# Attention in steps of two key tiles, q and k transposed on the host, and each engine's order written out

## The chip, the core and the metric

The kernel runs on one NeuronCore of a Trainium2 chip. Its time is the device time of one execution in microseconds, the median of the runs; lower is better. The engines are PE (TensorE), DVE (VectorE), ACT (ScalarE), POOL (GpSimd) and SP (SyncE, which here only issues DMAs); PEld in a profile is PE's loading of weights.

## The reference

Attention with a block mask over 4 batches of 8 heads, 768 positions and 64 columns a head, then a feed-forward network (FFN) over all 3072 tokens:

```python
def _attn_ref(q, k, v, sampled_blocks):
    B, H, S, D = q.shape
    scores = (1.0 / np.sqrt(D)) * np.matmul(q, k.transpose(0, 1, 3, 2))
    ...
    mask = np.abs(blk_i - blk_j) <= 1
    mask = mask | (blk_i == 0) | (blk_j == 0) | (blk_i == n_blocks - 1) | (blk_j == n_blocks - 1)
    ...
    scores = np.where(mask, scores, -1000000000.0)
    scores = scores - np.max(scores, axis=-1, keepdims=True)
    attn = np.exp(scores)
    attn = attn / (np.sum(attn, axis=-1, keepdims=True) + 1e-09)
    return np.matmul(attn, v)

def _moe_ref(x, w_in, w_out):
    h = x @ w_in
    g = h - np.tanh(h)
    return g @ w_out
```

Blocks are of 32 positions; where lines are left out, the block numbers are worked out and three sampled key blocks are allowed for each query block. The two weight matrices are 512 × 2048 and 2048 × 512.

## The kernel before

**Attention.** Two heads make a pair; there are 16. The scores are computed transposed, keys on partitions: for a key tile of 128 rows, PE multiplies it with all 768 queries (`qk_exp`, L270). Products keep fp32 accuracy by splitting each operand into a high part (rounded by ACT) and a low part (the rest), and the mask and the row maximum enter the product as 25 more rows. Four operand areas per pair (`sA` to `sD`, in one of three `slots`) hold these rows; the maxima for a query tile come from a product of its own (`smax`, L252), are reduced by DVE (L253), turned by PE (L258), negated (L260) and sent by DMA into a row of `sB` (L261), which the scores then need (L277).

For one key tile: PE writes the scores to PSUM (L276, L277), ACT takes the exponential to SBUF, `pe` (L279), ACT or DVE rounds it to fp16, `ph` (L289, L287), POOL or DVE subtracts it, `pl` (L291), and PE accumulates both with v (L306, L312, L313, eighteen multiplications). Of twelve key tiles of a pair, DVE takes two `ph` and one `pl`. After six key tiles DVE normalizes the head (`norm`, L321 to L325) and a finished pair is written to DRAM (`spill`).

q and k come untransposed. For each pair PE turns them with twelve transposes into PSUM (L192), ACT takes the high parts (L194), DVE the low parts (L195), and twelve DMAs of 192 KB (`dist`, L207) spread them over the operand areas. v is scaled by a power of two and split by ACT (L237) and DVE (L238).

**PSUM.** Of the eight banks, six form three buffers of 1024 columns (`big`: turned q and k, maxima, scores), and two are single banks (`one`: accumulators, small turns, the first FFN products).

**The FFN.** 96 units, each a tile of 512 tokens with 128 hidden columns: 12 multiplications into a PSUM bank (L527), tanh and a polynomial on ACT and DVE (L534 to L549), the low part on POOL (L550), 12 multiplications out (L559 to L561). Weights come as 64-bit words, converted by three DVE operations (L426, L429, L432) and split in two parts. The weights of the first three hidden tiles are converted during the attention; two more loads (L414, L418) are issued at the very start. Two units (`ffn.step`) are written inside the attention stage, on `one`.

**Order.** Every piece of work is put in a list with a time (`at`, L340), and the list is sorted; a scheduler then orders each engine's instructions by its own simulation, within the dependencies, so that the order on an engine isn't the order of the list.

## Time and profile before

| | |
|---|---|
| runs | 995.37, 996.8, 991.48 us; median 995.37 |
| the profiled execution | 990.7 us span |
| PE, DVE, ACT, POOL busy | 930.6, 742.5, 627.5, 458.4 us |
| DMA | 99.78 MB, 101 GB/s over the span |

The span reaches from the first to the last instruction of the profiled execution. The attention lasts to about 436 us, the FFN from there to the end. Shares of the whole span are means over both: what bounds the attention is to be read from its own stretches of time. The page's slices:

```profile
PE   5888998999899999878999999999999999999997
DVE  5699787888788888868999876766676666666664
ACT  1566787888688888745666665564565555555553
POOL 1566677777677777853454522222222222222221
PEclk9999999999999999998999999999999999999999
DMA  9988677677667777214451220210020000001001
```

Each digit is one of 40 slices of 24.8 us, in tenths. PE is the busiest in both stages; POOL's work is nearly all in the first 18 slices, where the attention is.

### The profile page before, as it was taken

The page shows a single profiled execution, that of the slowest core. Times are in us where ns is not written, and L with a number is a line of the kernel's source. Part 1 is how long each engine was busy: PE and PEld are TensorE (multiplying, and loading weights), DVE is VectorE, ACT ScalarE, POOL GpSimd, SP SyncE. Part 2 cuts the span into 40 slices and gives each one's busy share as a digit, 9 for nine tenths or more (in the row PEclk, how much of TensorE's full clock was granted, in tenths as well). Part 3 has the DMA queues.
Part 4 walks back from the last instruction along what each step waited for, and adds up shares of the span by engine and source line. Part 5 has one row for each costly group of instructions (what it writes and reads, how often), then busy time and mean ns, then how long its engine had stood idle before and what let it go on. Part 6 is the DMA issues. An engine that isn't in the chain of part 4 may idle for free.

```text
span 990.7 us, 18571 instructions
## 1 busy us (share of the span) xinstructions
PE 930.6 (94%) x7264; PEld 776.5 (78%) x7264; DVE 742.5 (75%) x1120; ACT 627.5 (63%) x943; POOL 458.4 (46%) x308
## 2 busy tenths in 40 slices
PE   5888998999899999878999999999999999999997
PEld 4666887888788888766878878888888888888885
DVE  5699787888788888868999876766676666666664
ACT  1566787888688888745666665564565555555553
POOL 1566677777677777853454522222222222222221
PEclk9999999999999999998999999999999999999999
DMA  9988677677667777214451220210020000001001
GB/s 234 253 228 200 158 165 161 153 167 172 137 160 168 175 165 182 85 32 154 128 187 50 79 75 11 94 35 12 1 75 1 1 22 22 1 1 43 1 1 42
DMA packets 74695, 99.78 MB, mean 101 GB/s; under 512 B 6008, under 2 KB 63544, under 8 KB 74608
## 3 DMA queue, kind: packets, MB, share of 16 engines
q1 hardware_dynamic: 74608, 98.60, 39.2%
q8 instruction: 57, 0.93, 0.4%
q14 instruction: 30, 0.25, 0.1%
HBM read 44.64 MB, written 15.20 MB: 60 GB/s over the span
## 4 chain that ended last, share of the span: by engine, by line
PE 70%; DMA 12%; DVE 9%; ACT 3%; issue 3%; SPq 1%; POOL 1%; ACTq 0%; DVEq 0%; POOLq 0%
PE pf L527 25%; PE pf L559 8%; PE pf L560 8%; PE pf L561 8%; DMA slot<-nm 7%; PE st L276 4%; PE st L277 4%; PE sm L252 3%; DVE mc L253 2%; PE av L313 2%; PE av L312 1%; DMA slot<-hiq 1%; PE av L306 1%; DMA slot<-hik 1%; DVE ph L287 1%
## 5 line engine op out<-in xcount | busy, mean ns | idle before, releaser
L291 POOL TENSOR_TENSOR pl<-pe,ph 128x768 f16<-128x768 f32 x173 | 290.6, 1693 | 132.1 <-ACT ph L289 80.9
L550 POOL TENSOR_TENSOR gl<-t,gh 128x512 fp32r<-128x512 f32 x96 | 124.1, 1293 | 362.9 <-ACT gh L549 304.9
L253 DVE TENSOR_REDUCE mc<-sm 128x1 f32<-128x768 f32 x192 | 181.2, 952 | 64.0 <-PE sm L252 62.6
L279 ACT ACTIVATE pe<-st 128x768 f32<-128x768 f32 x192 | 154.5, 807 | 86.6 <-PE st L277 77.7
L542 DVE TENSOR_TENSOR t<-t,pf 128x512 f32<-128x512 f32 x94 | 64.6, 687 | 123.8 <-ACT t L536 123.7
L276 PE MATMUL st<-slot 128*128 128x512 f32 (+1 forms) x384 | 144.6, 377 | 6.2 <-DVE mc L253 5.4
L277 PE MATMUL st<-slot 89*128 89x512 f32 (+1 forms) x384 | 127.9, 353 | 10.8 <-DMA slot<-nm 10.8
L549 ACT ACTIVATE gh<-t 128x512 fp32r<-128x512 f32 x96 | 60.6, 631 | 120.7 <-DVE t L546 120.7
L289 ACT ACTIVATE ph<-pe 128x768 f16<-128x768 f32 x154 | 129.6, 843 | 3.7
L313 PE MATMUL av<-vhl,pl 128*128 128x65 f16 x1152 | 129.3, 194 | 2.0 <-POOL pl L291 1.7
L312 PE MATMUL av<-vhl,ph 128*128 128x64 f16 x1152 | 129.0, 195 | 0.0
L306 PE MATMUL av<-vhl,ph 128*128 128x65 f16 x1152 | 128.5, 195 | 0.0
L252 PE MATMUL sm<-slot 88*128 88x512 f32 (+1 forms) x384 | 113.3, 381 | 13.5 <-DMA slot<-hiq 7.3
L313 PEld LDWEIGHTS <-pl 128*128 128x128 f16 x1152 | 107.0, 99 | 14.8 <-issue 8.2
L306 PEld LDWEIGHTS <-ph 128*128 128x128 f16 x1152 | 107.6, 97 | 4.4 <-issue 1.3
L312 PEld LDWEIGHTS <-ph 128*128 128x128 f16 x1152 | 108.3, 98 | 1.5 <-issue 0.8
L534 ACT ACTIVATE u<-pf 128x512 f32<-128x512 f32 x94 | 56.2, 598 | 82.0 <-PE pf L527 81.6
L276 PEld LDWEIGHTS st<-slot 128*128 128x128 f32 x384 | 75.4, 196 | 25.8 <-DVE mc L253 7.2
L277 PEld LDWEIGHTS st<-slot 89*128 89x128 f32 x384 | 76.1, 198 | 24.0 <-DMA slot<-nm 14.8
L252 PEld LDWEIGHTS sm<-slot 88*128 88x128 f32 x384 | 63.1, 204 | 17.8 <-issue 5.7
L546 DVE COPY_PREDICATED t<-mk,pf 128x512 f32<-128x512 int32 x94 | 69.8, 743 | 6.9 <-DVE pf L545 0.5
L559 PE MATMUL pf<-wx,gh 128*128 128x512 f32 x192 | 74.7, 389 | 0.0
(123 smaller groups left out, 1981.4 us busy)
## 6 DMA issues: line engine op xcount, KB each, us to landing
slot<-hik SPq DMA_DIRECT2D x64, 192.0 KB
slot<-hiq SPq DMA_DIRECT2D x64, 192.0 KB
stage<-w_in SPq DMA_DIRECT2D x13, 512.0 KB
stage<-w_out SPq DMA_DIRECT2D x13, 512.0 KB
rawk<-k SPq DMA_DIRECT2D x16, 384.0 KB
...
```

The source lines that it names most:

```text
L252: nc.tensor.matmul(pm[:, c], lhsT=sB[s][0:88, j, t * P : (t + 1) * P], rhs=sA[s][0:88, j, c], start=True, stop=True)
L253: maxed.append(nc.vector.tensor_reduce(out=mcs[h][:, t : t + 1], in_=pm[:, 0:S], op=ALU.max, axis=AX.X))
L276: nc.tensor.matmul(st[:, c], lhsT=sC[s][:, j, kc], rhs=sD[s][:, j, c], start=True, stop=False)
L277: nc.tensor.matmul(st[:, c], lhsT=sA[s][0:89, j, kc], rhs=sB[s][0:89, j, c], start=False, stop=True)
L279: nc.scalar.activation(out=pe, in_=st[:, 0:S], func=AF.Exp, scale=0.125)
L289: nc.scalar.activation(out=ph, in_=pe, func=AF.Copy)
L291: d = eng.tensor_tensor(out=pl, in0=pe, in1=ph, op=ALU.subtract)
L306: m = nc.tensor.matmul(o[:, to, :], lhsT=ph[:, c], rhs=vv[:, 0:65], start=(kt == 0 and t == 0), stop=False, skip_group_check=True)
L312: nc.tensor.matmul(o[:, to, 0:64], lhsT=ph[:, c], rhs=vv[:, 65:129], start=False, stop=False, skip_group_check=True)
L313: nc.tensor.matmul(o[:, to, :], lhsT=pl[:, c], rhs=vv[:, 0:65], start=False, stop=last, skip_group_check=True)
L527: nc.tensor.matmul(h, lhsT=w[:, cc], rhs=x[:, c, :], start=(k == 0), stop=(k == 3 * NCT - 1))
L559: nc.tensor.matmul(o, lhsT=gh[:, c], rhs=wo[0][ft], start=(ft == f0), stop=False)
```

## The change

The host hands over q and k already transposed, as one array of [pair, 128, 2, 768], and v in tile order. PE's transposes of q and k and their PSUM buffers go; ACT takes the high part of both from SBUF in one operation (L133), and POOL the low part, where DVE took it from PSUM (L141).

A step now takes two key tiles. Scores go to one fixed area of three banks (`pst`), maxima to another (`psm`), accumulators to one bank, small turns to one; each is a single buffer. The exponential (L256), the rounding (L260), the subtraction (L266) and the reduction of the maxima (L226) have 1536 columns; all rounding is on ACT and all subtraction on POOL. `pe` has two buffers, `ph` and `pl` four. Multiplications are as many as before, but for the columns at which they are cut. The accumulation of a step stands after the scores and the maxima of the step two later.

At the end of the stage, `in_order` chains every engine's instructions, SP's DMAs included, in the order of the list, so that the scheduler has no choice there. The conversion of the first weights is cut into its three operations, one a pair; `split_w` runs on DVE alone; the two loads of L414 and L418 move from the start to step 91; the first two FFN units use banks of `psm`. The output rows of a tile are adjacent. The first pair has paths of its own.

```diff
+def in_order(tc, start):
+
+    last = {}
+    for i in tc.nc.cur_bb.bb.instructions[start:]:
+        if i.engine in last:
+            tc.add_manual_dep(
+                i,
+                last[i.engine].name,
+                mybir.DependencyInfo(mybir.DependencyClass.NoSync, mybir.DependencyReason.DATA),
+                reason="order",
+            )
+        last[i.engine] = i
+
...
-        big = actx.enter_context(tc.tile_pool(name="ps_big", bufs=3, space=PSUM))
-        one = actx.enter_context(tc.tile_pool(name="ps_one", bufs=2, space=PSUM))
...
-        )
-        ffn.big, ffn.one = ps
...
+    ps = ctx.enter_context(tc.tile_pool(name="ps", bufs=1, space=PSUM))
+    pst = ps.tile([P, W2], F32, name="pst")
+    psm = ps.tile([P, W2], F32, name="psm")
+    pav = ps.tile([P, 512], F32, name="pav")
+    pmisc = ps.tile([P, 512], F32, name="pmisc")
...
+    def high(pr, x=None):
+        if pr == 1:
+            hms[pr] = [p2.tile([P, 1024], F32R, tag="wraw", name=f"hm1{x}")[:, 0:S] for x in range(2)]
+        elif pr not in hms:
+            t = p2.tile([P, 2, S], F32R, tag="hm", name=f"hm{pr}", bufs=1)
+            hms[pr] = [t[:, 0], t[:, 1], t.bitcast(F32)]
+        if pr > 1:
+            nc.scalar.activation(out=t, in_=raws[pr], func=AF.Copy)
+        else:
+            for x in range(2):
+                nc.scalar.activation(out=hms[pr][x], in_=raws[pr][:, x], func=AF.Copy)
+
+    def low(pr):
+        los[pr] = p2.tile([P, 2, S], F32R, tag="lo", name=f"lo{pr}", bufs=1)
+        if pr > 1:
+            nc.gpsimd.tensor_tensor(out=los[pr], in0=raws[pr], in1=hms[pr][2], op=ALU.subtract)
...
+    def direct(dst, x):
+        nc.vector.tensor_copy(out=dst[0][0:64, 0], in_=hms[0][x].bitcast(F32)[0:64])
+
+    def dist(pr, dst, r0, src, x, j):
+        nc.sync.dma_start(
+            out=dst[pr % NSLOT].bitcast(F32)[r0 : r0 + 64, j], in_=(src[pr][x] if src is hms else src[pr][:, x]).bitcast(F32)[64 * j : 64 * j + 64]
+        )
...
-    def prep_qk(pr, nm):
-        raw = loads[pr][0 if nm == "k" else 1]
-        hi = p2.tile([P, 2, HS], F32R, tag="hi" + nm, name=f"hi{nm}{pr}", bufs=1)
-        lo = p2.tile([P, 2 * HS], F32R, tag="lo" + nm, name=f"lo{nm}{pr}", bufs=1).rearrange("p (j c) -> p j c", j=2)
-        pt = big(f"pt{nm}{pr}")
-        for j in range(2):
-            for u in range(3):
-                c = (3 * j + u) * P
-                nc.tensor.transpose(pt[:, c : c + P], raw[:, j, 2 * u : 2 * u + 2, :].rearrange("p r d -> p (r d)"), ident)
-        ptv = pt[:, 0:S].rearrange("p (j c) -> p j c", j=2)
-        nc.scalar.activation(out=hi, in_=ptv, func=AF.Copy)
-        nc.vector.tensor_tensor(out=lo, in0=ptv, in1=hi.bitcast(F32), op=ALU.subtract)
-        hl[pr, nm] = hi, lo
...
-        pm = big(f"sm{h}_{t}")
-        for c in (slice(0, 512), slice(512, S)):
-            nc.tensor.matmul(pm[:, c], lhsT=sB[s][0:88, j, t * P : (t + 1) * P], rhs=sA[s][0:88, j, c], start=True, stop=True)
-        maxed.append(nc.vector.tensor_reduce(out=mcs[h][:, t : t + 1], in_=pm[:, 0:S], op=ALU.max, axis=AX.X))
...
+        for x in range(2):
+            t = 2 * i + x
+            for c in ((0, 512), (512, 768)) if x == 0 else ((0, 256), (256, 768)):
...
+    def maxima(h, i, ps=psm):
+        nc.vector.tensor_reduce(
+            out=mcs[h][:, 2 * i : 2 * i + 2], in_=ps.rearrange("p (x s) -> p x s", x=2), op=ALU.max, axis=AX.X
+        )
...
-        st = big(f"st{h}_{kt}")
-        kc = slice(kt * P, (kt + 1) * P)
-        for c in (slice(0, 512), slice(512, S)):
-            nc.tensor.matmul(st[:, c], lhsT=sC[s][:, j, kc], rhs=sD[s][:, j, c], start=True, stop=False)
-            nc.tensor.matmul(st[:, c], lhsT=sA[s][0:89, j, kc], rhs=sB[s][0:89, j, c], start=False, stop=True)
-        pe = p2.tile([P, S], F32, tag="pe", name=f"pe{h}_{kt}", bufs=4)
-        nc.scalar.activation(out=pe, in_=st[:, 0:S], func=AF.Exp, scale=0.125)
-        pes[h, kt] = pe
-
-    def split(h, kt):
-        pe = pes.pop((h, kt))
-        ph = p2.tile([P, S], F16, tag="ph", name=f"ph{h}_{kt}", bufs=PB)
-        pl = p2.tile([P, S], F16, tag="pl", name=f"pl{h}_{kt}", bufs=PB)
-        if (h * T + kt) % 12 in (PH_DVE if h < HPH else PH_DVE_END):
-            nc.vector.tensor_copy(out=ph, in_=pe)
-        else:
-            nc.scalar.activation(out=ph, in_=pe, func=AF.Copy)
-        eng = nc.vector if (h * T + kt) % 12 in (PL_DVE if h < HPL else PL_DVE_END) else nc.gpsimd
-        d = eng.tensor_tensor(out=pl, in0=pe, in1=ph, op=ALU.subtract)
-        plin[h, kt] = d
...
+        for x in range(2):
+            kc = slice((2 * i + x) * P, (2 * i + x + 1) * P)
+            for c in ((0, 512), (512, 768)) if x == 0 else ((0, 256), (256, 768)):
+                o = pst[:, x * S + c[0] : x * S + c[1]]
+                q = slice(*c)
+                nc.tensor.matmul(o, lhsT=sC[s][:, j, kc], rhs=sD[s][:, j, q], start=True, stop=False)
+                nc.tensor.matmul(o, lhsT=sA[s][0:89, j, kc], rhs=sB[s][0:89, j, q], start=False, stop=True)
+
+    def expo(s_):
+        pes[s_] = p2.tile([P, W2], F32, tag="pe", name=f"pe{s_}", bufs=2)
+        nc.scalar.activation(out=pes[s_], in_=pst, func=AF.Exp, scale=0.125)
+
+    def p_high(s_):
+        ph = p2.tile([P, W2], F16, tag="ph", name=f"ph{s_}", bufs=4)
+        nc.scalar.activation(out=ph, in_=pes[s_], func=AF.Copy)
+        phs[s_] = ph
+
+    def p_low(s_):
+        ph = phs[s_]
+        pl = p2.tile([P, W2], F16, tag="pl", name=f"pl{s_}", bufs=4)
+        nc.gpsimd.tensor_tensor(out=pl, in0=pes.pop(s_), in1=ph, op=ALU.subtract)
+        phs[s_] = ph, pl
...
+    def accum(s_):
...
+        ph, pl = phs.pop(s_)
+        for x in range(2):
+            kt = 2 * i + x
...
+                nc.tensor.matmul(oav[:, t, :], lhsT=ph[:, c], rhs=vv[:, 0:65], start=(kt == 0 and t == 0), stop=False, skip_group_check=True)
...
+    k = -76
+    for c, j in ((CD[:2], 0), (AB, 1), (CD[2:], 0)):
+        for d in c:
+            at(k, dist, 0, *d, j)
...
+    for s in range(NSTEP):
+        at(s, scores, s)
+        at(s + 0.02, expo, s)
+        at(s + 0.12, p_high, s)
+        at(s + 0.2, p_low, s)
+        at(s + 2.5, accum, s)
+    for h in range(NHEAD):
+        if h >= 2:
+            for i in range(3):
+                at(3 * h - 6 + i + 0.1, smax, h, i)
+                at(3 * h - 6 + i + 0.11, maxima, h, i)
+            at(3 * h - 3 + 0.05, turn_max, h)
+            at(3 * h - 3 + 0.07, neg_max, h)
+        at(3 * h + 5.03, norm, h)
...
+        load_w(nc, wraw[m, ft], w_in, w_out, m, ft)
...
+    for x in range(6 * NPRE):
+        m, ft, n = "io"[x // 3 % 2], x // 6, x % 3
+        s = 6 * x + 10 if x < 13 else 77 + x
+        if n == 0:
+            at(s - 4.5 if x < 15 else 87, load_pre, m, ft)
+        at(s + 0.04, convert_pre, m, ft, n)
...
+    ffn.one = one
     for j in range(CT):
-        at(X0 + DX * j, x_first, j)
+        at(84.3 + 0.4 * j, x_load, j)
+        at(90.06 + j, x_turn, j)
...
-        at(F0 + DF * i + 2, ffn.split_w, i)
+        at(90.2 + 0.4 * i if i < 2 else 94.3, ffn.fetch_w, i)
+        at(92.04 + i if i < 2 else 96.3, ffn.split_w, i)
...
+        at(91.5 + 0.3 * i, ffn.stage_w, i)
...
+        at(95.6 + i, ffn.step)
     ev.sort(key=lambda e: e[:2])
     for _, _, f, args in ev:
         f(*args)
+    in_order(tc, start)
...
-            self.parts(lo.bitcast(F32), hi, lo, self.nc.vector if ft < 2 and x else self.nc.gpsimd)
+            self.parts(lo.bitcast(F32), hi, lo, self.nc.vector)
...
-                nc.sync.dma_start(out=self.out[b * S : (b + 1) * S, :].rearrange("(p t) d -> t p d", t=T)[t], in_=ob)
+                nc.sync.dma_start(out=self.out[b * S + t * P : b * S + (t + 1) * P, :], in_=ob)
...
-    block = (col % P * T + np.array(TORD)[col // P]) // BLK
+    block = col // BLK
...
+    kq = np.stack([inputs["k"], inputs["q"]]).reshape(2, NPAIR, 2, S, D).transpose(1, 2, 4, 0, 3).reshape(NPAIR, P, 2, S)
+    vt = inputs["v"].reshape(NPAIR, 2, T, P, D).transpose(0, 3, 1, 2, 4).reshape(NPAIR, P, 2 * T * D)
```

PE in the middle of the attention. Before, around the scores of a key tile (`st`), with head and tile in the names (`ptk11` is pair 11's turned k, `pmt20` head 20's turned maxima, `av18` an accumulator):

```order
L312 MATMUL av18_4616<-vhl0_103,ph18_5_4702 128x64
L313 LDWEIGHTS pl18_5_4703
L313 MATMUL av18_4616<-vhl0_103,pl18_5_4703 128x65
L306 LDWEIGHTS ph18_5_4702
L306 MATMUL av18_4616<-vhl0_103,ph18_5_4702 128x65
L192 MATMUL ptk11_4764<-ident_64,rawk11_4187 128x128
L258 MATMUL pmt20_4690<-ident_64,mc20_4514 6x128
L192 MATMUL ptk11_4764<-ident_64,rawk11_4187 128x128 x5
L312 LDWEIGHTS ph18_5_4702
L312 MATMUL av18_4616<-vhl0_103,ph18_5_4702 128x64
```

The transposes stand between multiplications of one accumulation. After, the end of an accumulation (of step 1), and the scores and maxima that follow it:

```order
L283 MATMUL pav_102<-vhl0_104,pl1_268 128x65
L251 MATMUL pst_100<-slot0_73 128x512
L252 MATMUL pst_100<-slot0_73 128x512
L251 MATMUL pst_100<-slot0_73 128x256
L252 MATMUL pst_100<-slot0_73 128x256
L251 MATMUL pst_100<-slot0_73 128x256
L252 MATMUL pst_100<-slot0_73 128x256
L251 MATMUL pst_100<-slot0_73 128x512
L252 MATMUL pst_100<-slot0_73 128x512
L216 MATMUL psm_101<-slot1_74 128x512
L216 MATMUL psm_101<-slot1_74 128x256 x2
L216 MATMUL psm_101<-slot1_74 128x512
```

The transposes are gone, and scores and maxima of two tiles stand in one run, then the next accumulation.

POOL in the first pairs. Before, it does nothing in the attention but subtractions (head and key tile in the names):

```order
L291 TENSOR_TENSOR pl8_2_2234<-pe8_2_2160,ph8_2_2233 128x768
L291 TENSOR_TENSOR pl8_3_2249<-pe8_3_2175,ph8_3_2248 128x768
L291 TENSOR_TENSOR pl8_4_2307<-pe8_4_2231,ph8_4_2306 128x768
L291 TENSOR_TENSOR pl8_5_2337<-pe8_5_2246,ph8_5_2336 128x768
L291 TENSOR_TENSOR pl9_0_2389<-pe9_0_2304,ph9_0_2388 128x768
```

After, with the low part of a pair's q and k among them (steps in the names of `pl`, pairs in those of `lo`):

```order
L141 TENSOR_TENSOR lo4_883<-raw4_690,hm4_814 128x1536
L266 TENSOR_TENSOR pl12_944<-pe12_929,ph12_941 128x1536
L266 TENSOR_TENSOR pl13_1003<-pe13_993,ph13_1001 128x1536
L266 TENSOR_TENSOR pl14_1069<-pe14_1054,ph14_1067 128x1536
L266 TENSOR_TENSOR pl15_1134<-pe15_1120,ph15_1132 128x1536
L266 TENSOR_TENSOR pl16_1197<-pe16_1182,ph16_1192 128x1536
L266 TENSOR_TENSOR pl17_1261<-pe17_1243,ph17_1259 128x1536
L141 TENSOR_TENSOR lo5_1263<-raw5_1071,hm5_1194 128x1536
L266 TENSOR_TENSOR pl18_1324<-pe18_1309,ph18_1321 128x1536
```

Once in six steps the low part stands between two subtractions. ACT some pairs later, after:

```order
L260 ACTIVATE ph22_1573<-pe22_1562 128x1536
L133 ACTIVATE hm6_1575<-raw6_1451 128x1536
L256 ACTIVATE pe23_1624<-pst_100 128x1536
L260 ACTIVATE ph23_1640<-pe23_1624 128x1536
L256 ACTIVATE pe24_1692<-pst_100 128x1536
L260 ACTIVATE ph24_1704<-pe24_1692 128x1536
L197 ACTIVATE vhl2_106<-rawv5_1423,sb5_1631 128x12x64
L256 ACTIVATE pe25_1756<-pst_100 128x1536
L260 ACTIVATE ph25_1764<-pe25_1756 128x1536
L256 ACTIVATE pe26_1817<-pst_100 128x1536
```

The high part of the next q and k stands between a rounding and the next exponential, and so does, two steps later, the scaled v.

The end of the attention on PE. Before, around the first FFN products (`h0_0`, `h0_1`) and the first turn of the FFN (`pf6`):

```order
L312 MATMUL av31_7628<-vhl0_103,ph31_3_7624 128x64
L527 MATMUL h0_0_7665<-slot1_74,slot2_75 128x512 x12
L313 LDWEIGHTS pl31_3_7625
...
L313 MATMUL av31_7628<-vhl0_103,pl31_5_7700 128x65
L527 MATMUL h0_1_7739<-slot1_74,slot2_75 128x512 x12
L441 MATMUL pf6_7859<-ident_64,slot1_74 128x128 x4
L527 MATMUL pf4_7857<-slot1_74,slot2_75 128x512 x12
```

After, with the step's number in `pl`:

```order
L283 MATMUL pav_102<-vhl0_104,pl93_6066 128x65
L583 MATMUL psm_101<-slot1_74,slot2_75 128x512 x12
L281 LDWEIGHTS ph94_6116
...
L283 MATMUL pav_102<-vhl0_104,pl94_6118 128x65
L583 MATMUL psm_101<-slot1_74,slot2_75 128x512 x12
L281 LDWEIGHTS ph95_6173
...
L283 MATMUL pav_102<-vhl0_104,pl95_6175 128x65
L497 MATMUL pf6_6400<-ident_64,slot1_74 128x128 x4
L583 MATMUL pf4_6398<-slot1_74,slot2_75 128x512 x12
```

Both units stand ahead of the last accumulation, where the second stood behind it.

SP's queue at the start, after; the load of the pair 2's q and k (`raw2`) is its row 21:

```order
L150 DMA slot1_74<-hm10_147 64x768
L150 DMA slot1_74<-hm11_148 64x768
L150 DMA slot0_73<-hm0_132 64x768 x2
L150 DMA slot0_73<-lo0_138 64x768 x2
L150 DMA slot1_74<-hm10_147 64x768
L150 DMA slot1_74<-hm11_148 64x768
L175 DMA slot2_75<-st_sb_111 24x2x768
L175 DMA slot2_75<-mk_112 24x2x768
L120 DMA raw2_199<-qk 128x1536
L150 DMA slot1_74<-hm10_147 64x768
L150 DMA slot1_74<-hm11_148 64x768
L150 DMA slot1_74<-lo1_185 64x768 x2
```

Loads, fills and distributions of the pairs 0 and 1 stand ahead of it.

More of the change, by code (lines that the diff above doesn't have):

```diff
@@ L44 @@
 NPRE = 3
[L45 removed]
 NV = 3
[L47 to L63 removed]
+XF = 8
+NH0 = 2
+HIMASK = -4096
 THR2 = 0.16
@@ L130, in load @@
-    def load(pr, which="kqv", first=None):
-        b, hp = divmod(pr, H // 2)
-        r = loads.setdefault(pr, [])
-        for nm, src in ((n, x) for n, x in (("k", k), ("q", q), ("v", v)) if n in which):
-            t = p2.tile([P, 2, T, D], F32, tag="raw" + nm, name=f"raw{nm}{pr}", bufs=2)
-            d = nc.sync.dma_start(out=t, in_=src[b, 2 * hp : 2 * hp + 2].rearrange("h (p t) d -> p h t d", t=T))
-            r.append(t)
-            if pr <= 3 and first is not None:
-                after(first, d)
```

375 lines of the change are left out of this document (186 added, 189 removed).

## The prediction, made before the changed kernel ran

> **What bounds the kernel now.** I read the busy shares and the chain first, to see which engine and which of its waits set the end; then windows of one steady pair, to get the pace; then single rows.
>
> ```profile
> span 990.7 us, 18571 instructions
> PE 70%; DMA 12%; DVE 9%; ACT 3%; issue 3%; SPq 1%; POOL 1%; ACTq 0%; DVEq 0%; POOLq 0%
> 0.00:60.00 60.00, 42.58 (x342) 33.89 (x343) 40.17 (x63) 26.27 (x33) 22.80 (x20) 1.00 0.91 232
> 60.00:120.00 60.00, 51.83 (x603) 42.53 (x604) 52.44 (x78) 40.19 (x51) 39.46 (x22) 0.94 0.78 197
> ...
> 285.00:309.00 24.00, 22.74 (x305) 19.63 (x304) 19.64 (x29) 19.50 (x26) 18.08 (x11) 1.00 0.71 167
> 285.00:309.00 24.00, 9.68 (x12) 1.00 0.71 167
> ```
>
> A window row gives the stretch, its length, the busy time of PE, PEld, DVE, ACT and POOL, then the granted PE clock, the DMA share and GB/s; the last row is the same stretch counting only the exponentials (L279). Twelve exponentials are one pair of heads, so a pair takes 24.0 us in the middle of the attention, PE is busy for 22.7 of them, and POOL only for 18.1. In the first 60 us DMA is the limit (0.91 of its engines, 232 GB/s); the row of 60 to 120 still shows it at 0.78.
>
> ```profile
> L291 POOL TENSOR_TENSOR pl<-pe,ph 128x768 f16<-128x768 f32 x173 | 290.6, 1693 | 132.1 <-ACT ph L289 80.9
> L550 POOL TENSOR_TENSOR gl<-t,gh 128x512 fp32r<-128x512 f32 x96 | 124.1, 1293 | 362.9 <-ACT gh L549 304.9
> L253 DVE TENSOR_REDUCE mc<-sm 128x1 f32<-128x768 f32 x192 | 181.2, 952 | 64.0 <-PE sm L252 62.6
> L279 ACT ACTIVATE pe<-st 128x768 f32<-128x768 f32 x192 | 154.5, 807 | 86.6 <-PE st L277 77.7
> L289 ACT ACTIVATE ph<-pe 128x768 f16<-128x768 f32 x154 | 129.6, 843 | 3.7
> L534 ACT ACTIVATE u<-pf 128x512 f32<-128x512 f32 x94 | 56.2, 598 | 82.0 <-PE pf L527 81.6
> ```
>
> These are groups: line, operation and shape, then total busy us and mean ns of one, then the idle time before them and who ended it. ACT and DVE wait for PE; POOL waits for ACT. So PE sets the pace of the steady attention, with 1.3 us of gaps per pair.
>
> **PE's part.** The timeline of PE, start and length:
>
> ```profile
> 257.47 0.48 PE L276 MATMUL st<-slot 128*128 128x512 f32 x1
> ...
> 258.26 0.51 PE L252 MATMUL sm<-slot 88*128 88x512 f32 x2
> 258.61 0.21 PE L313 MATMUL av<-vhl,pl 128*128 128x65 f16 x1
> ...
> 259.30 0.71 PE L192 MATMUL ptk<-ident,rawk 128*128 128x128 f32 x5
> 259.84 0.19 PE L312 MATMUL av<-vhl,ph 128*128 128x64 f16 x1
> ...
> 431.55 0.20 PE L313 MATMUL av<-vhl,pl 128*128 128x65 f16 x1
> ...
> 432.05 0.19 PE L306 MATMUL av<-vhl,ph 128*128 128x65 f16 x1
> 432.08 0.19 PE L312 MATMUL av<-vhl,ph 128*128 128x64 f16 x1
> ```
>
> Recorded lengths overlap, so I take start to start. Scores of one key tile take 258.26 − 257.47 = 0.79 us, maxima 0.35, and the eighteen accumulating matmuls from 431.55 to 432.08 take 18/17 of 0.53, or 0.56. A step of two tiles is therefore 2 × (0.79 + 0.35 + 0.56) = 3.40 us, and a pair of six steps 20.4. The change issues exactly these multiplications again, with other column cuts. Five transposes last 0.54 us (259.30 to 259.84), so the twelve that go take 1.3 us per pair. If PE still set the pace, a pair would fall from 24.0 to about 20.4 + 0.3 for the two small turns + the gaps of today, 1.3: 22.0. That would be 2 us × about 14.5 steady pairs = 29 us.
>
> **What else can set the pace.** Two rows of single lines, with minimum, median and maximum ns and the first and last start:
>
> ```profile
> L279 ACT ACTIVATE pe<-st x192: 784/811/815, 31.6 to 431.6; 128x768 f32<-128x768 f32 x192
> L237 ACT ACTIVATE vhl<-rawv,sb x16: 933/936/947, 34.9 to 403.9; 128x768 f16<-128x768 f32 x16
> ```
>
> ACT: the slope of one element is (807 − 598)/256 = 0.82 ns, so a 1536-column exponential is 807 + 768 × 0.82 = 1.43 us and its rounded copy 0.843 + 0.63 = 1.47. Six steps are 17.4, the one high part of q and k adds 1.47, the scaled v 0.94: 19.8 of ACT, below PE. DVE: six reductions at 2 × 0.95 less one start, about 1.8 each, 10.8 instead of today's 11.4, and it loses its rounded copies, its low parts of q, k and one subtraction; DVE is no bound. Moving those copies to ACT is hidden under the waits of 86.6 us that ACT has before L279.
>
> POOL is the resource that changes most. It took eleven of twelve 768-column subtractions; now it takes every one, as six of 1536 columns, and the low part of q and k besides. The before trace has no 1536-column POOL operation. From below, its slope is that between its two shapes, (1693 − 1293)/256 = 1.56 ns, so 1.69 + 768 × 1.56 = 2.89; the undisturbed minimum of 1.635 (its row is below) against the same 1.293 makes 1.34 ns and 2.66. From above it is twice the undisturbed median, 3.30. I take 3.1, nearer to the upper end, because two operations of its own line are the nearest row, less one start. The low part has the types of L550: from below 1.293 + 1024 × 1.34 = 2.66, from above 3 × 1.293 = 3.88; I take 3.4 by the same reasoning. POOL per pair: 6 × 3.1 + 3.4 = 22.0, bounds 18.6 to 23.7. POOL thus becomes as long as PE's 22.0, and comes ahead of it with any loss.
>
> The Trainium skill, "GPSIMD Engine Reference", section "3.1 Elementwise — side-by-side cycle accounting", gives 4497 ns for a two-input fp32 operation of 2048 columns, which scaled to 1536 is an estimate of 3.37 us; by that the sum would be 6 × 3.37 + 3.4 = 23.6 per pair, and no run here has that shape.
>
> **Two losses on POOL.** First, the buffers. There are two `pe` tiles, so exponential s+2 waits for subtraction s, and then 1.43 + 1.47 must pass on ACT before subtraction s+2 can start, while POOL has only subtraction s+1, 3.1, to do: even, with 0.2 to spare. The 1.47 of the q and k copy and the 0.94 of v, once a pair each, stand on ACT between a rounded copy and the next exponential, and in this kernel nothing may overtake them. Up to 2.4 us per pair would show as a hole on POOL; its 3.4 us low part, which needs no exponential, fills part. From 0 to 2.4, I take 1.2.
>
> Second, a lock between DVE and POOL:
>
> ```profile
> L291 POOL TENSOR_TENSOR pl<-pe,ph x173: 1635/1650/2622, 33.4 to 433.6; 128x768 f16<-128x768 f32 x173
> L238 DVE SCALAR_TENSOR_TENSOR vhl<-rawv,sb,vhl x16: 1019/1020/2397, 37.8 to 405.5; 128x768 f16<-128x768 f32 x16
> 60.78 2.62 POOL L291 TENSOR_TENSOR pl<-pe,ph 128x768 f16<-128x768 f32 x1 [5.15 <-ACT ph L289]
> 61.22 0.68 DVE L432 SCALAR_TENSOR_TENSOR cvto<-rawo,cvto 128x512 int32<-128x512 int32 x1
> 61.83 2.40 DVE L238 SCALAR_TENSOR_TENSOR vhl<-rawv,sb,vhl 128x768 f16<-128x768 f32 x1
> ```
>
> A subtraction that starts at 60.78 while DVE is at operations with two SBUF inputs lasts 2.62 instead of 1.65: it ends 1.5 after DVE's at 61.90. DVE's v low part, 1.02 alone, then lasts 2.40, to 64.23: 0.83 after POOL is done at 63.40. They take turns. In the changed kernel DVE keeps one such v low part per pair and one part of a weight conversion (0.68), so up to 1.02 + 0.68 = 1.7 us of POOL per pair goes to them; where they fall into POOL's holes it is nothing. I take half, 0.8. DVE's wait, up to 3 us behind a 1536-column operation, holds the reduction queued behind it, and so PE's next maxima; DVE, busy for 19.6 of 24 us now and for less then, has room to catch up.
>
> The Trainium skill, "SBUF — State Buffer", section "🔬 SBUF: two separate sides", says that GpSimd and such a DVE operation hold a shared port pair exclusively for the whole instruction, whichever starts first. This trace agrees (2.62 against 1.65); by the rule the whole 1.7 would be lost in every pair, 0.9 × 14.5 = 13 us more than I take, and without it nothing.
>
> Sum per pair: 22.0 + 1.2 + 0.8 = 24.0, against 24.0 now. So the 29 us of PE are, by my reading, eaten by POOL: the steady stretch comes out even.
>
> **Front.** Pair 0 needs fewer steps before its first exponential: no transposes, no 1 MB of weights at the head of the queue (at 232 GB/s that is 4.5 us), so I expect it at 24 to 27 instead of 31.6. But the second exponential stands behind the high part of pair 2 on ACT, whose load is row 21 of the queue. Up to it stand three loads of q and k (0.79 MB each by their shapes), fourteen distributed pieces (0.197), six fills (0.147), v (0.39) and the tables (0.08): 6.5 MB, 28 us at 232 GB/s, so the second exponential comes at about 33 to 36. Distribution traffic per pair is the same, twelve pieces of 192 KB. I take 0, from −6 to +6.
>
> **Tail.**
>
> ```profile
> 431.58 0.81 ACT L279 ACTIVATE pe<-st 128x768 f32<-128x768 f32 x1 [1.25 <-DVE rs L321]
> 434.25 4.57 PE L527 MATMUL h<-slot,slot 128*128 128x512 f32 x12 [1.97 <-DVE xq L325]
> 443.18 0.73 DVE L546 COPY_PREDICATED t<-mk,h 128x512 f32<-128x512 int32 x1
> 447.60 0.60 ACT L534 ACTIVATE u<-h 128x512 f32<-128x512 f32 x1 [3.02 <-PE h L527]
> 452.47 1.09 PE L441 MATMUL pf<-ident,slot 128*128 128x128 f32 x4 [4.91 <-issue]
> 452.48 0.69 DVE L426 TENSOR_SCALAR pf<-stage 128x512 int32<-128x512 int32 x1
> 434.00:439.00 5.00, 4.75 (x23) 3.68 (x24) 2.01 (x2) 0.14 (x1) 1.20 (x1) 0.66 0.00 0
> ```
>
> Today unit 0 of the FFN waits for the last but one normalization (1.97 us), runs at a clock of 0.66 and takes 4.57; unit 1 must wait for head 31's normalization and ends at 447.6, and the first transposes and the first conversion come at 452.5, 20.9 us after the last exponential. After the change both units stand between the last accumulations and use the bank of the maxima, free by then. Last exponential + 1.43 + 1.47 + 3.1 is +6.0; two port waits behind DVE's weight splits, about +2; accumulation +1.1: +9.1. Then either the turn follows at once (11.8 us saved), or, if both units' element work on DVE (twice five operations of 0.7 as L546's) comes first, 7 us later, and 4.8 are saved. I take 9, nearer to the first, since unit 0's element work can run beside the accumulations. From there the FFN is untouched, and its pace passes the shift on.
>
> Sum: 0 + 0 − 9 against the span of 990.7 gives 981.7. The median of the runs, 995.37, lies 4.7 above that span, outside it or by run; I add this: 986.4.
>
> **Rivals.**
> (A) The forecast, POOL about level with today's pace: 986.
> (B) POOL's long operation is cheap (2.66 for both shapes, 18.6 per pair) or the port turns fall into holes. Then PE bounds at 22.0: −29 − 9 plus 4 for losses at the front, 961. For it: POOL's 1.3 ns slope from its own rows. Against it: rows of two dtypes can't give a clean slope.
> (C) Slower: POOL at its upper price, 6 × 3.2 + 3.6 = 22.8, plus 1.6 of holes and 1.2 of turns, 25.6 per pair. That is +1.6 × 14.5 = 23, − 9: 1009. It decides where POOL's total with losses passes 24.6 per pair, for there the tail's 9 us are spent. For it: 2.62 and 2.40 above. Against it: POOL sat idle 132.1 us before L291, some of which was slack that can be used. PE's gaps, 24.0 − 20.7, cost nothing as long as its clock stays above 0.86; the row of 434 to 439 shows 0.66 after a wait of 2 us, and if that happened after each hole, C would come sooner.
> (D) The pace is even and the tail's gain does not arrive, because the conversions and not the units set the FFN's start: 995.
>
> **How the numbers follow.** A 0.42, B 0.24, C 0.24, D 0.10. The predicted time is A's 986.4. B reaches below 961 only if the holes vanish as well, C above 1013 only at both upper prices, so 958 to 1013 holds eight in ten. A's own range, from half the tail gain lost (+4.5) to a POOL 0.4 us per pair cheaper (−5.8), is 981 to 991. 0.5%, or 5 us, is about what a measurement can tell from no change: below 990.4 lie B and most of A, 0.54; above 1000.4 C and a little of D, 0.26; the rest is 0.20.
>
> **What would show it.** Right: POOL busy above 21 of each 24 us, its 1536-column mean between 2.9 and 3.3, ACT's exponentials waiting for POOL's subtraction instead of PE, and the transposes ahead of unit 2 some 12 us after the last exponential, not 20.9. Wrong: PE at over 95% in steady windows (B), a pair over 25 us or stretched v low parts of 3 us and more in every pair (C), a first exponential before 25 followed by a hole beyond 12 us (front mis-sized), or a first conversion still 20 us behind the last exponential (D).

## The result and the profile after

The change makes the kernel slower: 1032.76 us (1023.37 to 1044.67, 4 runs) against 993.42, ratio 1.0315, interval 1.0266 to 1.0364. Two of its four runs, 1039.29 and 1044.67, fell in a slower state of the chip at a lower clock; the ratio and its interval leave them out. The profiled execution has a span of 1021.6 us, 30.9 more than before. Starts of exponentials and of the first conversion of the FFN, from the two timelines, divide that:

| stretch | before | after | difference |
|---|---|---|---|
| start to exponential of tile 24, step 12 | 90.1 | 95.7 | +5.6 |
| from there to tile 168, step 84 (twelve pairs) | 297.1 | 321.1 | +24.0 |
| to the last exponential | 44.4 | 44.2 | −0.1 |
| to the first conversion | 20.9 | 19.6 | −1.2 |
| to the end | 538.2 | 540.9 | +2.6 |

Tiles and steps are counted from 0. So nearly four fifths of the loss lie in the steady attention: 26.8 us per pair against 24.8 (the 24.0 of the prediction was one of the quicker pairs). One window of 240 us, before and then after, with the columns of the prediction's windows:

```profile
120.00:360.00 240.00, 226.51 (x2982) 196.37 (x2979) 192.83 (x295) 193.78 (x246) 177.43 (x108) 0.99 0.72 160
```

```profile
120.00:360.00 240.00, 209.36 (x2618) 178.02 (x2618) 179.00 (x175) 172.23 (x124) 201.18 (x63) 0.90 0.62 159
```

PE's share fell from 94% to 87%, POOL's rose from 74% to 84%, and no engine is full. PE's granted clock fell from 0.99 to 0.90, so part of PE's 87% is slower work. The costs, in the views by group and by single line:

```profile
L266 POOL TENSOR_TENSOR pl<-pe,ph 128x1536 f16<-128x1536 f32 x96 | 308.9, 3226 | 72.5 <-ACT ph L260 52.4
...
L266 POOL TENSOR_TENSOR pl<-pe,ph x96: 3095/3122/3847, 32.6 to 464.2; 128x1536 f16<-128x1536 f32 x96
L141 POOL TENSOR_TENSOR lo<-raw,hm x14: 3472/3488/3507, 47.7 to 394.2; 128x1536 fp32r<-128x1536 f32 x14
L473 DVE TENSOR_SCALAR cvti<-rawi x3: 3211/3220/3226, 85.5 to 408.1; 128x512 int32<-128x512 int32 x3
L477 DVE SCALAR_TENSOR_TENSOR cvto<-rawo,cvto x3: 2992/3322/3481, 199.4 to 452.8; 128x512 int32<-128x512 int32 x3
L473 DVE TENSOR_SCALAR pf<-stage x26: 680/689/706, 480.7 to 592.6; 128x512 int32<-128x512 int32 x26
L201 DVE SCALAR_TENSOR_TENSOR vhl<-rawv,sb,vhl x16: 1010/2818/3926, 30.7 to 420.7; 128x768 f16<-128x768 f32 x16
```

POOL's prices are what was forecast (3.12 and 3.49). New are DVE's lengths: a conversion operation, 0.69 in the FFN, takes 3.2 to 3.5 us in the attention in the median, v's low part 2.8, where it took 1.02 before. What one such wait does, in the timelines of POOL, DVE, PE and ACT (start, length, idle time before and its releaser):

```profile
157.08 9.96 POOL L266 TENSOR_TENSOR pl<-pe,ph 128x1536 f16<-128x1536 f32 x3
...
157.38 3.63 DVE L201 SCALAR_TENSOR_TENSOR vhl<-rawv,sb,vhl 128x768 f16<-128x768 f32 x1 [1.33 <-ACT vhl L197]
160.94 1.74 DVE L225 TENSOR_REDUCE mc<-psm 128x2 f32<-128x1536 f32 x1
...
162.74 1.01 PE L216 MATMUL psm<-slot 88*128 88x512 f32 x4 [2.32 <-DVE mc L225]
...
167.95 1.45 ACT L256 ACTIVATE pe<-pst 128x1536 f32<-128x1536 f32 x1 [4.48 <-PE pst L252]
...
171.05 3.12 POOL L266 TENSOR_TENSOR pl<-pe,ph 128x1536 f16<-128x1536 f32 x1 [4.01 <-ACT ph L260]
```

DVE's v low part starts just after a subtraction and gets on only when that is over; the reduction behind it starts 3.6 us late; PE's next maxima wait for the single buffer that this reduction reads, and behind them, in the fixed order, the accumulation and the next scores; ACT waits 4.48, and in the end POOL itself 4.01. After its wait PE is also slower for a while. The window rows before and behind the wait:

```profile
155.00:160.40 5.40, 5.39 (x69) 4.36 (x65) 4.07 (x2) 5.14 (x4) 5.27 (x3) 1.00 0.84 199
163.00:168.00 5.00, 5.00 (x50) 4.40 (x50) 2.32 (x2) 0.52 (x2) 4.04 (x2) 0.66 0.66 150
```

The granted clock is 0.66 there instead of 1.00, and from the first multiplication of an accumulation to the last one of the scores behind it PE takes 3.8 us instead of 2.6.

### The profile page after: what moved, and what is told of

Read it like the earlier page. It is cut to its first block, busy times and chain, and to the rows that moved or that the text cites. A ratio compares the mean times of both kernels' runs of the same rounds, so it can differ in the third digit from the quotient of the medians.

```text
span 1021.6 us, 17486 instructions
## 1 busy us (share of the span) xinstructions
PE 923.3 (90%) x7072; PEld 768.4 (75%) x7072; DVE 721.3 (71%) x939; ACT 630.7 (62%) x775; POOL 527.2 (52%) x245
## 4 chain that ended last, share of the span: by engine, by line
PE 61%; DVE 19%; ACT 6%; issue 4%; POOL 1%; DMA 1%; SPq 0%; DVEq 0%; ACTq 0%; POOLq 0%
PE pf L583 23%; PE pf L615 8%; PE pf L616 8%; PE pf L617 8%; DVE mc L225 6%; PE psm L216 3%; ACT pe L256 3%; PE pst L251 3%; DVE vhl L201 3%; PE pst L252 3%; PE pav L281 2%; PE pav L283 1%; POOL pl L266 1%; PE pav L282 1%; DVE am L179 1%
## 5 line engine op out<-in xcount | busy, mean ns | idle before, releaser
L266 POOL TENSOR_TENSOR pl<-pe,ph 128x1536 f16<-128x1536 f32 x96 | 308.9, 3226 | 72.5 <-ACT ph L260 52.4
L256 ACT ACTIVATE pe<-pst 128x1536 f32<-128x1536 f32 x96 | 138.7, 1445 | 119.3 <-PE pst L252 96.1
L225 DVE TENSOR_REDUCE mc<-psm 128x2 f32<-128x1536 f32 x94 | 164.7, 1753 | 39.2 <-PE psm L216 39.0
L251 PE MATMUL pst<-slot 128*128 128x512 f32 (+1 forms) x384 | 143.6, 392 | 14.5 <-ACT pe L256 13.6
L216 PE MATMUL psm<-slot 88*128 88x512 f32 (+1 forms) x376 | 96.1, 382 | 55.2 <-DVE mc L225 44.5
L260 ACT ACTIVATE ph<-pe 128x1536 f16<-128x1536 f32 x96 | 142.6, 1485 | 2.9
L283 PE MATMUL pav<-vhl,pl 128*128 128x65 f16 x1152 | 130.3, 201 | 5.0 <-POOL pl L266 4.8
L252 PE MATMUL pst<-slot 89*128 89x512 f32 (+1 forms) x384 | 132.9, 364 | 0.0
L281 PE MATMUL pav<-vhl,ph 128*128 128x65 f16 x1152 | 131.7, 203 | 0.5 <-DVE xq L294 0.5
L282 PE MATMUL pav<-vhl,ph 128*128 128x64 f16 x1152 | 131.2, 204 | 0.0
```

What stands on the lines that cost most here:

```text
L216: nc.tensor.matmul(ps[:, x * S + c[0] : x * S + c[1]], lhsT=sB[s][0:88, j, t * P : (t + 1) * P], rhs=sA[s][0:88, j, c[0] : c[1]], start=Tr ...
L225: nc.vector.tensor_reduce(out=mcs[h][:, 2 * i : 2 * i + 2], in_=ps.rearrange("p (x s) -> p x s", x=2), op=ALU.max, axis=AX.X)
L251: nc.tensor.matmul(o, lhsT=sC[s][:, j, kc], rhs=sD[s][:, j, q], start=True, stop=False)
L252: nc.tensor.matmul(o, lhsT=sA[s][0:89, j, kc], rhs=sB[s][0:89, j, q], start=False, stop=True)
L256: nc.scalar.activation(out=pes[s_], in_=pst, func=AF.Exp, scale=0.125)
L266: nc.gpsimd.tensor_tensor(out=pl, in0=pes.pop(s_), in1=ph, op=ALU.subtract)
```

## The experiments

Theory **port**: the DVE operations that need what POOL's subtraction holds make the holes. Rivals: **loops** (single or double buffers in a fixed order leave no slack), POOL's rate, PE's clock, the two ends. The results first; the pace is from step 12 to step 84, and each ratio is to runs of the kernel before that were taken with the experiment. A pace is read from one execution. The eight of e2 lie 13.6 us apart, about 1 us per pair if all of it fell in these twelve pairs, so differences of a few tenths are not shown by a pace alone.

| run | us per pair | last exponential | span | median us | ratio to before, interval |
|---|---|---|---|---|---|
| the change | 26.8 | 461.1 | 1021.6 | 1032.76 | 1.0315, 1.0266–1.0364 |
| e1 no conversions, no v low | 23.8 | 419.6 | 982.3 | 985.29 | 0.9875, 0.9773–0.9978 |
| e2 no conversions | 25.8 | 449.1 | 1007.7 | 999.58 | 1.0018, 0.9987–1.0049 |
| e3 subtractions halved | 27.2 | 461.1 | 1018.7 | 1021.27 | 1.0236, 1.0133–1.0339 |
| e4 both placed later | 25.8 | 443.1 | 1009.1 | 1013.73 | 1.0160, 1.0039–1.0282 |
| e5 conversions through PSUM, in halves | 25.4 | 441.2 | 1000.8 | 1004.74 | 1.0104, 1.0071–1.0137 |
| e6 e1, three `pe` | 23.9 | 424.8 | 983.6 | 984.16 | 0.9869, 0.9765–0.9973 |
| e7 both ends | 27.9 | 466.4 | 1020.8 | 1021.03 | 1.0239, 1.0131–1.0347 |
| e8 a first combination | 29.5 | 488.0 | 1041.6 | 1045.14 | 1.0491, 1.0403–1.0579 |
| e9 e1, later accumulation | 24.5 | 429.4 | 989.8 | 991.02 | 0.9990, 0.9963–1.0017 |
| e10 e5, v low later | 26.1 | 451.4 | 1009.8 | 1010.35 | 1.0175, 1.0121–1.0228 |
| e11 e10 and the front | 26.1 | 440.1 | 997.8 | 1000.95 | 1.0110, 1.0033–1.0187 |
| e12 e5, no v low | 24.1 | 420.0 | 982.7 | 983.49 | 0.9856, 0.9793–0.9919 |
| e13 both through PSUM, front | 24.6 | 429.3 | 987.2 | 991.42 | 0.9919, 0.9894–0.9944 |
| e14 e13, no units | 24.7 | 431.0 | 991.7 | 993.55 | 0.9989, 0.9954–1.0025 |
| e15 e1, with the slack of e6 and e9 | 21.9 | 390.5 | 953.4 | 956.71 | 0.9588, 0.9525–0.9651 |
| e16 the change, with the slack of e6 and e9 | 25.1 | 431.1 | 991.8 | 999.64 | 1.0016, 0.9978–1.0055 |
| e17 e13, with the slack of e6 and e9 | 22.7 | 404.0 | 963.8 | 965.96 | 0.9694, 0.9653–0.9736 |

**The port.** First both kinds of DVE operation were left out, then the conversions alone; zeros stand in for what they would have computed.

```diff
-        at(x + 7.03, v_low, pr)
...
-        convert_part(nc, n, wraw[m, ft], cvt[m, ft], cvt[m, ft])
         if n == 2:
-            nc.sync.dma_start(out=wt[m, ft], in_=cvt[m, ft].bitcast(F32))
+            nc.sync.dma_start(out=wt[m, ft], in_=zero)
```

> Leaves out the low part of v (set to zero once) and the three conversion operations of the first weights during the attention (zeros are stored in their place): the two kinds of DVE operation whose median rose from 1.02 to 2.82 us and from 0.69 to about 3.3 us. Port theory (each waits for POOL's whole 1536-column operation, and the reduction queued behind it holds PE's maxima): the stretch from step 12 to step 84, 26.8 us per pair, falls to 22 to 23.5, and the time from 1023 to 975 to 990. Rival, single score and maxima buffers in a fixed order with a low PE clock: the pace stays over 25.5 and the time over 1010. If only the operations' own lengths counted (1.7 us per pair), the time would be near 1000.

> Leaves out only the conversion operations (18 of them, 13 in the steady part), the low part of v stays. Port theory: the larger half of the gain of the run without both, 25 to 30 us, since each conversion held DVE for 3.3 us against 2.8 for v; time 993 to 1000. Rival, single buffers: under 8 us gain, above 1015.

Without both, the pace falls by 3.0 us per pair, where their own lengths make 1.7. PE's clock in the window of 120 to 360 is 0.99 again, so its fall to 0.90 came with the holes. The time of e1 is as the port theory had it, its pace 0.3 above. Without the conversions alone the pace falls by 1.0; the ratio falls by 0.030 of e1's 0.044, the span of the profiled execution by 14 of 39 us, and that execution is the longest of e2's eight. Both kinds count, and e2 doesn't settle how they divide.

e3 cuts the subtraction (`pl[:, 0:768]`, `pl[:, 768:1536]`), e4 moves the two operations behind their step's reduction:

```diff
-        at(x + 7.03, v_low, pr)
+        at(x + 7.12, v_low, pr)
...
-        at(s + 0.04, convert_pre, m, ft, n)
+        at(s + 0.12, convert_pre, m, ft, n)
```

> POOL's subtractions cut into two of 768 columns, nothing else. Port theory: DVE's wait is bounded by 1.65 instead of 3.1 us, so the conversion's median falls from 3.3 to about 1.9 and v's low part from 2.8 to about 1.9; about 1.2 us saved at 28 places, less 7 extra starts of 0.2 us per pair on POOL, which has holes: time 995 to 1010. Rival, POOL's own rate is the bound: 1.3 us per pair more, about 1040.

> The two kinds of locking DVE operation stand directly behind the reduction of their step instead of ahead of it; lengths and waits for POOL stay as they are. If the reduction queued behind the wait is what reaches PE: the hole at each of some 28 places shrinks by up to the reduction's 1.75 us, time 985 to 1010. If POOL's lost time is what counts: within 5 us of 1023.

In e3 DVE's waits shrank as expected (v's low part to 1.85, the conversions to 1.07 to 1.33 in the median), and still the pace did not fall (27.2) and the span fell by only 2.9; the time lies in neither forecast. Two halves of 1.69 for one operation of 3.23 cost POOL 0.9 us in six steps, and what else took the gain was not followed. In e4 the waits nearly went (v 1.45, conversions 0.42 to 1.0), and only 1.0 us per pair came of it; the time missed its forecast, also because the first conversion of the FFN came 25.7 us after the last exponential instead of 19.6. The waits between 95 and 380 us (engine and line, for whom, us in total, times, longest), first of the changed kernel, then of e4, say what held the pace instead:

```profile
PE psm L216 <- DVE mc L225: 35.8, 21, 2.6
...
ACT pe L256 <- POOL pl L266: 14.3, 9, 3.1
```

```profile
ACT pe L256 <- POOL pl L266: 38.9, 11, 3.6
...
PE pav L283 <- POOL pl L266: 20.2, 11, 1.8
```

PE's wait for DVE's reduction, 35.8 us, is gone from e4's list, and waits for POOL have come up in its place: those of the two loops below. So DVE's wait is not all.

e5 keeps the conversions ahead of their step's reduction, with the intermediate in PSUM, in halves; all twelve halves of three operations lie in the steady part, where thirteen of the eighteen operations lay:

```diff
+        t = pmisc[:, 256:512].bitcast(I32)
+        nc.vector.tensor_scalar(
+            out=t, in0=w[:, :, 1], scalar1=3, scalar2=0x3FFFFFF8, op0=ALU.logical_shift_left, op1=ALU.bitwise_and
+        )
...
+            out=cvt[m, ft][:, part], in0=w[:, :, 0], scalar=29, in1=t, op0=ALU.logical_shift_right, op1=ALU.bitwise_or
```

> The conversions stay at the place that they had, but in halves of 256 words and with the intermediate in 256 free columns of the bank of small turns, so that none has two SBUF inputs; all is computed. Port theory: each of these DVE operations lasts 0.4 to 0.7 us instead of 3.3, v's low part stays at about 3; the time is that of the run without conversions plus 1.2 us of DVE per pair, 998 to 1006. If any DVE work at this place were the cause: 1015 or more.

This tests the port most directly. POOL and DVE in e5's timelines:

```profile
261.81 3.11 POOL L266 TENSOR_TENSOR pl<-pe,ph 128x1536 f16<-128x1536 f32 x1 [0.82 <-ACT ph L260]
...
262.00 0.42 DVE L417 TENSOR_SCALAR pmisc<-rawo 128x256 int32<-128x256 int32 x1
262.45 0.43 DVE L420 SCALAR_TENSOR_TENSOR pmisc<-rawo,pmisc 128x256 int32<-128x256 int32 x1
262.92 0.42 DVE L423 SCALAR_TENSOR_TENSOR cvto<-rawo,pmisc 128x256 int32<-128x256 int32 x1
```

The same arithmetic runs beside the subtraction, which isn't stretched either (3.11); the pace, 25.4, is no worse than without conversions (25.8). The Trainium skill, "SBUF — State Buffer", section "🔬 SBUF: two separate sides", has this as a port pair that GpSimd shares with DVE operations that have two SBUF inputs or run in a two-port mode; the trace agrees.

What v costs: e10 is e5 with v's low part placed as in e4, e12 is e5 without it, e13 computes it in three parts with the high part copied to PSUM by ACT:

```diff
+        nc.scalar.activation(out=pv, in_=vv[:, :, 0:64], func=AF.Copy)
         nc.vector.scalar_tensor_tensor(
-            out=vv[:, :, 65:129], in0=rawv[pr], scalar=sbs[pr], in1=vv[:, :, 0:64], op0=ALU.mult, op1=ALU.subtract
+            out=vv[:, :, 65:129], in0=rawv[pr][:, 4 * x : 4 * x + 4], scalar=sbs[pr], in1=pv, op0=ALU.mult, op1=ALU.subtract
```

> Conversions through PSUM as in the run of that kind (25.4 us per pair), and v's low part behind its step's reduction. All is computed. Theory: v's wait for POOL no longer holds a reduction, and takes a port turn of about 1 us: 24.2 to 24.8 per pair, 985 to 995 us. If POOL's lost turn is all that v costs: 25.2 or more, 1000 or more.

> Conversions through PSUM (25.4 us per pair with v's low part at its place), and the low part of v left out (zero). If v's turn at the port is the rest: 23.7 to 24.2 per pair, as without both, 980 to 987. If DVE's 1.3 us of conversions per pair also cost: 24.5 or more, 990 or more.

> All is computed. Conversions through PSUM, and v's low part in three parts with the high part copied to PSUM by ACT first, so that neither has two SBUF inputs; the front as in the earlier run. Port theory: 23.8 to 24.6 per pair (1.3 us more of ACT), step 12 at 87 to 89: 972 to 984, faster than the kernel before. If the place of work on DVE and not the port costs: 25.5 or more, 995 or more.

e12 comes to 24.1, near e1: 1.3 us of DVE work per pair costs at most some tenths. v's one operation therefore costs 1.3 us per pair at its own place (25.4 − 24.1) and 2.0 where DVE hardly waits for POOL (26.1; its median there is 1.41). The mean subtraction is 3.21 and 3.23 in these two, against 3.11 in e1: some 0.7 us of POOL per pair, which came out as two to three times as much. e10 missed its forecast; its waits are like e4's: none of PE for the reduction, and those for POOL (38.4 and 20.2 us) in its place. Through PSUM v costs about 0.5 (e13 against e12), ACT's three added copies included.

**The loops.** 23.8 is still above POOL's 22.2 (6 × 3.12 + 3.49). e6 has three `pe` buffers on top of e1 (and three of `pl` instead of four, for room), e9 the accumulation a step later on top of e1, e15 both on top of e1, e16 both on top of the changed kernel.

```diff
-        pes[s_] = p2.tile([P, W2], F32, tag="pe", name=f"pe{s_}", bufs=2)
+        pes[s_] = p2.tile([P, W2], F32, tag="pe", name=f"pe{s_}", bufs=3)
...
-        at(s + 2.5, accum, s)
+        at(s + 3.5, accum, s)
```

> The run without both kinds of locking operation, with three exponential buffers for two (and three for four of the low part, to make room). Theory on what is left, 23.8 us per pair there against 22.2 of POOL work: exponential s+2 waits for subtraction s, behind the low part of q and k, 2.8 us a pair. Then the pace falls to 22.3 to 23.0 per pair and the time to 965 to 977. Rival, single PSUM buffers for scores and maxima: the pace stays at 23.5 or more, the time at 982 or more.

> The run without both kinds of locking operation (23.8 us per pair), with the accumulation, normalization and spill one step later in the list. Theory on the rest between 22.2 us of POOL work and 23.8: PE's scores of step s+3 stand behind the accumulation of step s, which waits for POOL's subtraction of step s, so POOL waits for itself around PE and ACT. Then 22.3 to 23.2 per pair and 966 to 977 us. Rival, the single score buffer (scores, exponential, scores) with the q and k copy between: 23.5 or more and 980 or more.

> Neither locking operation, three exponential buffers and the accumulation one step later, both together. If the two loops (exponential behind subtraction, scores behind accumulation behind subtraction) each hold 23.8 by themselves: 22.3 to 23.0 per pair, 965 to 975. If the single score buffer with the in-order q and k copy holds it: 23.5 or more, 980 or more.

> The changed kernel with only the slack: three exponential buffers (three of the low part) and the accumulation, normalization and spill one step later; conversions and v's low part as the change has them. All is computed. If the port's waits cost mainly because the loops have no slack: POOL's 22.2 plus its lost turns of 1 to 1.7 us, 23.2 to 24.2 per pair, 978 to 992. If DVE's waits reach PE all the same, through the reduction queued behind them and the single buffer of maxima: 25.5 or more, 1005 or more.

Each alone gave nothing, as the rival of the single score buffer had it; both give 2 us per pair, which that rival can't explain. The waits between 95 and 380 us show the exchange, first in e1, then in e6:

```profile
ACT pe L259 <- POOL pl L269: 34.0, 12, 2.8
...
PE pav L286 <- POOL pl L269: 22.2, 12, 1.9
```

```profile
ACT pe L259 <- PE pst L255: 49.1, 48, 3.9
...
PE pav L286 <- POOL pl L269: 22.3, 12, 1.9
```

In e1 both loops show: ACT waits for POOL, and PE waits for POOL ahead of the accumulation. With three buffers (e6) ACT's wait for POOL is gone from the list, PE's is there as before, and ACT waits for PE instead, 49.1 us for 15.9. In e9 it is the other way round: PE's wait is gone, ACT's 34.0 stays. In e15 POOL has no hole left, and the pace is its work (21.9 for a sum of 22.2, as most operations start 0.03 to 0.07 us before the record of the one ahead ends):

```profile
120.00:360.00 240.00, 230.88 (x3212) 199.65 (x3210) 154.57 (x199) 213.78 (x154) 240.00 (x78) 1.00 0.74 196
```

e16 fell between its two outcomes, at 25.1: slack recovers 1.7 of the 4.9 us by which 26.8 stands above 21.9, and without the two kinds of DVE operation the same slack reaches 21.9.

**The ends.** e7 moves pair 2's load and four pieces of pair 0 ahead of the first maxima's DMA, and at the end unit 1 behind the last accumulation, in one of the scores' banks, with the third split of weights ahead of unit 0; e14 is e13 without units in the attention.

```diff
-            at(y - 3.7, load_qk, pr)
+            at(y - 3.7 if pr > 2 else -68.8, load_qk, pr)
...
-        at(95.6 + i, ffn.step)
+        at(95.6 + 2.5 * i, ffn.step)
```

> The changed kernel with other places in the list at both ends: the load of pair 2's q and k and the four second-head pieces of pair 0 ahead of the first maxima's DMA on SP, and, at the end, unit 1 in the bank of the scores and behind the last accumulation and normalization, the third weight split ahead of unit 0. All is computed. Theory on the ends: SP waits 7 us for the first maxima with 12 DMAs behind it, so exponential 1 comes 6 to 10 us sooner than 40.3, and step 12 3 to 9 us sooner than 95.7; the first conversion comes 12 to 15 us after the last exponential instead of 19.6. Time 1005 to 1015. If the front is bound by bytes, step 12 stays at 94 to 96; if the FFN's start hangs on the conversions' own chain, the tail stays over 18.

> The same with the front of the run of both ends (step 12 at 87.2 there for 95.7). All is computed. If pace and front are independent: 6 to 9 us below the run without it, 978 to 988, faster than the kernel before. If the front's gain is lost again in the steady part, as in the run of both ends: no gain.

> The same, with no FFN unit inside the attention stage. Theory on the tail: the conversions wait for the attention's PSUM, so for the last unit's element work; without units the first conversion comes 9 to 11 us after the last exponential instead of 19, and the two units then cost 6 to 8 of that again: 0 to 4 us faster than the run before. If the conversions hung on the weights' loads: no change in that distance.

The front's place was right: the second exponential came at 33.4 for 40.3, step 12 at 87.2 for 95.7. In e7 the steady part gave it back (27.9 per pair); in e11, where conversions no longer meet POOL, 9.5 us of it arrived at step 12 and 11.2 at the last exponential. In e13, with the same front, step 12 came at 94.4, against 87 to 89 expected: between steps 10 and 11 ACT's copy of q and k (L133, at 88.5) waited 4.73 us for a DMA. Why the DMA came later there wasn't followed. The tail of e7 fell from 19.6 to 16.3, less than expected: there too the first conversion comes right behind unit 1's last element operation. Without units (e14) it comes 9.4 us after the last exponential (19.3 in e13), but the units then stand in the FFN, and the time is no better.

**Combinations.** e8 put e5 at the later place, e4's v, three `pe` buffers and e7 together:

> All is computed: conversions through PSUM and behind their step's reduction, v's low part behind its reduction, three exponential buffers (three of the low part), front and tail as in the run before. Port and buffer theories together: pace 22.7 to 24 per pair, time 955 to 980, faster than the kernel before the change. Rival, v's low part alone still sets a hole of 2 us per pair and POOL bounds: 24.5 to 25 per pair, 985 to 995.

It missed by far. The waits of e8 say part of why:

```profile
PE pmisc L184 <- DVE cvti L424: 15.5, 5, 3.1
...
PE pmisc L184 <- DVE cvto L424: 12.4, 4, 3.1
```

At the later place the conversions stand between DVE's reduction and PE's matrix product for v's scale (L184), which writes the same PSUM tile: PE waits up to 3.1 us a time. In e5, ahead of the reduction, the same wait is at most 0.7. The 27.9 us are 2.9 per pair in this window, about half of what e8 lies above its forecast; the rest wasn't followed. e17 is e13 with the slack of e6 and e9:

> All is computed. No DVE operation with two SBUF inputs in the attention (conversions and v's low part through PSUM), three exponential buffers, the accumulation one step later, the front as in the earlier run. POOL bound at 22.2 per pair plus little: 22.2 to 23.2 per pair, 958 to 972, faster than both kernels. If ACT, with 1.3 us more per pair, sets holes again: 24 or more, 980 or more.

```profile
120.00:360.00 240.00, 222.52 (x3095) 190.40 (x3095) 173.76 (x254) 217.48 (x179) 232.16 (x75) 1.00 0.72 191
```

With POOL at 97% and 22.7 per pair it computes everything and beats both kernels: 965.96 us, 0.9694 of before (0.9653 to 0.9736).

## Why the prediction was wrong, step by step

**PE's part** was right. With all waits gone, e15 runs a pair in 21.9 with PE busy for 96% of the window; PE doesn't stand in the way of 22.0.

**POOL's prices** were right: 3.12 for 3.1 and 3.49 for 3.4, 22.2 per pair for 22.0, and e15 shows POOL's work as the bound. The Trainium skill's figure in "GPSIMD Engine Reference", section "3.1 Elementwise — side-by-side cycle accounting", scaled to an estimate of 3.37 us, was too high for the subtraction, whose second input and output are fp16 (3.12), and a little low for that of q and k, all fp32 (3.49).

**The holes from the buffers** were priced at 1.2 and came to 1.6 (e1's 23.8 − 22.2), or 1.9 against e15's 21.9. Only one of the two loops was seen: that the scores three steps on stand behind an accumulation that waits for the subtraction was missed.

**The lock is the step that failed.** It was priced by POOL's lost time, 0.8 of at most 1.7 us, with the words that DVE "has room to catch up". It cost 3.0 (e1), so a pair took 26.8 for the 24.0 of the sum. As the pair before took 24.8 and not 24.0, a right sum of 24.0 would have meant a gain in the steady part and not an even pace. DVE had the room on the average, but its wait of 3 us stands in a chain without a spare buffer: reduction, maxima, accumulation, scores. And a lost turn of POOL is not only its length: with no slack in the loops it returned as 1.3 to 2.0 us per pair for v's one operation. Rival C, with a chance of 0.24, had the direction and its signs (a pair over 25, v's low parts of 3 us, 2.8 in the median here), but not the path: it took POOL at a higher price than was measured (22.8 for 22.2) and the lock as 1.2 us of lost turns. Its 25.6 us per pair fell 1.2 short, and its 1009 was too low.

**The front** was just within its bounds of −6 to +6 at step 12 (+5.6), but the second exponential was not where it was put: at 40.3 and not at 33 to 36, 16 us behind the first, which is the prediction's own sign of a mis-sized front. SP, in the fixed order, waits from 11.5 to 18.4 us for the first maxima (`nm`), with twelve DMAs and then pair 2's load behind it:

```profile
10.96 0.58 SPq L124 DMA_DIRECT2D rawv<-v  x1
18.42 0.78 SPq L238 DMA_DIRECT2D slot<-nm  x1
...
29.23 0.79 SPq L120 DMA_DIRECT2D raw<-qk  x1
```

**The tail** gave 1.2 of the 9 forecast. Unit 1 did not run beside unit 0's element work: it waited for its end, and the last normalization and the conversions stood behind unit 1's:

```profile
470.40 4.62 PE L583 MATMUL psm<-slot,slot 128*128 128x512 f32 x12 [3.74 <-DVE t L602]
...
480.13 0.56 DVE L294 TENSOR_TENSOR xq<-pav,rs 128x384 f32<-128x384 f32 x1
480.72 0.69 DVE L473 TENSOR_SCALAR pf<-stage 128x512 int32<-128x512 int32 x1
```

That is the outcome of rival D, a first conversion still about 20 us behind the last exponential, but not its reason: the units did set the FFN's start, as e14 shows, where it came after 9.4 us without them.

**What stays open:** the 2.6 us that the FFN itself takes longer are not clear of scatter, as the same stretch takes 537 to 543 us in the experiments that leave the FFN as it is. The slower clock lengthens the one hole shown above by 1.2 us; in three of the eight 30 us windows from 120 to 360 it lies at 0.83 or 0.84, below the 0.86 under which the prediction expected a cost, and how much it adds over all pairs was not tried by itself. Nor is it shown whether and why v's low part costs more behind the reduction (e10) than ahead of it (e5): 0.7 us per pair, with intervals of the time that overlap.
